# Two relus on ScalarE in place of a copy and a maximum, a fixed VectorE order for the last experts, and a shorter softmax for two tiles

## The chip, the cores and the metric

The kernel runs on one core of a Trainium2 chip. The metric is the time of one execution in microseconds of device time. The engines are called as in the profile: PE is TensorE (matmuls and transposes), PEld its weight load, DVE is VectorE, ACT is ScalarE, POOL is GpSimd, SP is SyncE, which issues most of the DMA transfers.

## The reference

Three stages follow each other: an attention with 4 sink columns and a window of 128, a dense layer with a leaky relu, and a layer of 8 experts of which each token uses one.

```python
scores = scale * np.matmul(q, k.transpose(0, 1, 3, 2))       # 2 x 8 heads, 768 tokens, 64 each; scale 1/8
scores = np.where(is_sink | in_window, scores, -1e9)
a = np.exp(scores - np.max(scores, axis=-1, keepdims=True))
a = a / (np.sum(a, axis=-1, keepdims=True) + 1e-9)
x = heads_together(np.matmul(a, v))                          # 1536 tokens x 512

h = x @ w_in                                                 # 512 -> 2048, weights arrive as float64
x = np.maximum(0.01 * h, h) @ w_out                          # 2048 -> 512

expert = np.argmax(x @ w_gate, axis=1)                       # 8 experts, at most 384 tokens each
h = np.maximum(x_e @ w1[e], 0.0)                             # 512 -> 1024
out = gate_weight * (h @ w2[e])                              # 1024 -> 512
```

## The kernel before

One program does all three stages, with the stages laid over each other.

**Attention.** The 1536 tokens are 12 tiles of 128. The first two tiles are "plain": for each of four units (a tile and a group of four heads) `qk_plain` (L630) transposes k and q on PE into one PSUM tile `kps`, copies q with ACT to `qp` (L640) and k with DVE to the two zero-padded halves `kz` (L643, two copies of 64 partitions). `scores_plain` (L646) multiplies them on top of a mask `mp`, takes the negated maximum of the raw scores on DVE (L662) and multiplies it with the scale (L663). `exps_plain` (L667) applies the scale inside the exponential (L674) and keeps the sums `su`. `norm_plain` (L679) makes 1/(su + 1e-9) on DVE for each half of the heads (L684, L685), and POOL multiplies the probabilities with it. The other ten tiles go through a class with a ring of keys: there DVE writes the mask into the scores (L538), takes the maximum (L539), makes the reciprocal of the sum (L220, L221) and prepares parts of q, k and the output (L148, L176, L196, L311), ACT makes the exponential (L213), POOL scales it (L223) and makes low parts (L148, L203, L232).

**Dense layer.** The class `FFN` works on 6 blocks of 256 tokens, each over 16 slices f of 128 hidden columns. `first` (L833) computes a slice hps in PSUM, `leak` (L845) applies the leaky relu, `second` (L867) adds the slice's part of the output into y. `second` of a slice is issued two slices later (`LAG` = 2). In block 0 the weights are still raw 8-byte words: for each f DVE turns two tiles of them (`rawi`, `rawo`) into fp32 tiles `cvt` with three operations each (L782, L786, L792), 96 conversions in all. `convert` gives them a lower priority than the rest, so they fill the gaps between the other DVE operations. The remaining attention tiles run during block 0. PSUM holds one buffer for hps, so `first` of the next slice begins when `leak` has read this one. Blocks 1 to 5 use split weights `wh` and `wl` that were made in block 0 (L812 on ACT, L813 on POOL).

`leak` in all blocks:

```python
g = self.p["g"].tile([P, N], F32, tag="g", name="g")
nc.scalar.activation(g, ps, AF.Copy, scale=0.01)              # L852
nc.vector.tensor_tensor(out=g, in0=ps, in1=g, op=ALU.max)     # L853
```

**Experts.** Tokens are scattered into `places` in DRAM by expert. For each group of at most 384 tokens the class `Experts` loads tokens `xg` and weights `craw`, splits the weights into high and low parts `cw` (L1140, L1142 and L1144), transposes tokens (`turn`, L1235), splits them (`x_parts`: L1241 on ACT, L1242 on DVE), copies gate weight and target row of each token from `xg` to `gt` (L1243, DVE, 128x2), and runs the two products (`up_one` L1272, `turn_one` L1286 to L1289, `down` L1299). `out` (L1302) multiplies with the gate weight (L1307) and POOL issues the indirect DMA (L1308). The groups that follow the first ones run under a test of the token count; the last four, with few tokens, run as `lone` (L1318), one after the other, in the arm at L1419 to L1424.

**Order.** PE, SP, ACT and POOL issue in program order (`ORDERED`, with `manual_schedule`). The order of DVE is set by a scheduler from priorities and its own estimate of readiness. Every engine takes its instructions strictly in the order that results.

Of the kernel before, what the change touches and what calls it, by code (L numbers as in the profile page):

```python
# [8 lines left out]
F32 = mybir.dt.float32  # L9
F32R = mybir.dt.float32r  # L10
BF16 = mybir.dt.bfloat16
I32 = mybir.dt.int32
AF = mybir.ActivationFunctionType
ALU = mybir.AluOpType
# [4 lines left out]
P = 128  # L19
# [3 lines left out]
ET = mybir.EngineType  # L23
ORDERED = {ET.PE, ET.SP, ET.Activation, ET.Pool}
# [363 lines left out]
class RingAttention(Attention):  # L388
# [16 lines left out]
    def setup(self):  # L405
        nc = self.nc
        c = self.p["ac"]
# [5 lines left out]
        fill = NEG  # L413
# [4 lines left out]
        for t in range(self.plain):  # L418

            m = self.p["c"].tile([P, (t + 1) * P], BF16, tag="c", name="mp")  # L420
            nc.gpsimd.memset(m, 0.0)
            for x in range(t + 1):
                self.keep_mask(m[:, x * P:(x + 1) * P], (t - x) * P, 0 if x else self.n_sink, fill / self.scale)
            self.mp.append(m)
            for g in range(self.NG):
                q = self.p["c"].tile([P, 2, P], F32, tag="c", name="qp")
                k = self.p["c"].tile([P, 2, 2, P], F32, tag="c", name="kz")
                for e in range(2):
                    nc.vector.memset(k[64 - 64 * e:128 - 64 * e, e], 0.0)
                self.qk[t, g] = q, k  # L430
# [200 lines left out]
    def qk_plain(self, t, g):  # L631


        nc = self.nc
        ps = self.p["ps"].tile([P, 4, P], F32, tag="att", name="kps")
        for n, (nm, pr) in enumerate(("kq"[n // 2], n % 2) for n in range(4)):
            x = self.heads(t, g, nm)[:, 2 * pr:2 * pr + 2, :]
            nc.tensor.transpose(ps[:, n, :], x.rearrange("p a d -> p (a d)"), self.ident)
        q, k = self.qk[t, g]
        nc.scalar.copy(q, ps[:, 2:4, :])  # L640
        for e in range(2):
            d = slice(64 * e, 64 * e + 64)
            nc.vector.tensor_copy(k[d, e], ps[d, 0:2, :])  # L643

    def scores_plain(self, t, g):

        nc = self.nc
        n = t + 1
        mx = self.p["sm"].tile([P, 2, 2], F32, tag="mx", name="mx")
        pss = []  # L650
        for e in range(2):
            if (t * self.NG + g) % 2:
                ps = self.p["psy"].tile([P, 2, n, P], F32, tag=f"y{e}", name="sps")
            else:
                ps = self.p[("psh", "psc")[e]].tile([P, 2, n, P], F32, tag="hu"[e], name="sps")
            for pr in range(2):
                for x in range(n):
                    nc.tensor.matmul(ps[:, pr, x, :], lhsT=self.ident_b, rhs=self.mp[t][:, x * P:(x + 1) * P],
                                     start=True, stop=False)
                    nc.tensor.matmul(ps[:, pr, x, :], lhsT=self.qk[t, g][0][:, pr, :],  # L660
                                     rhs=self.qk[x, g][1][:, e, pr, :], start=False, stop=True)
            nc.vector.reduce_max(mx[:, e, :], ps.rearrange("p a n c -> p a (n c)"), axis=AX.X, negate=True)  # L662
            nc.vector.tensor_scalar(out=mx[:, e, :], in0=mx[:, e, :], scalar1=self.scale, scalar2=None, op0=ALU.mult)  # L663
            pss.append(ps)
        self.pu[t, g] = (pss, mx)

    def exps_plain(self, t, g):  # L667
        pss, mx = self.pu[t, g]
        su = self.p["sm"].tile([P, 2, 2], F32, tag="su", name="su")
        pms = []  # L670
        for e, ps in enumerate(pss):
            pm = self.p["c"].tile([P, 2, (t + 1) * P], F32, tag="c", name="pm")
            for pr in range(2):
                self.nc.scalar.activation(pm[:, pr, :], ps[:, pr].rearrange("p n c -> p (n c)"), AF.Exp,  # L674
                                          bias=mx[:, e, pr:pr + 1], scale=self.scale, accum_out=su[:, e, pr:pr + 1])
            pms.append(pm)
        self.pu[t, g] = (pms, su)

    def norm_plain(self, t, g):  # L679
        nc = self.nc  # L680
        pms, su = self.pu[t, g]
        ri = self.p["sm"].tile([P, 2, 2], F32, tag="ri", name="ri")
        for e, pm in enumerate(pms):
            nc.vector.tensor_scalar(out=ri[:, e], in0=su[:, e], scalar1=1.0e-9, scalar2=None, op0=ALU.add)  # L684
            nc.vector.reciprocal(ri[:, e], ri[:, e])  # L685
            nc.gpsimd.tensor_tensor(out=pm, in0=pm, in1=ri[:, e].unsqueeze(2).to_broadcast(list(pm.shape)), op=ALU.mult)

    def trans_plain(self, t, g):
# [35 lines left out]
class FFN:  # L724
# [10 lines left out]
    N = 256  # L735
# [111 lines left out]
    def leak(self, j, f):  # L847

        nc, N = self.nc, self.N
        ps = self.g[j, f]  # L850
        g = self.p["g"].tile([P, N], F32, tag="g", name="g")
        nc.scalar.activation(g, ps, AF.Copy, scale=0.01)  # L852
        nc.vector.tensor_tensor(out=g, in0=ps, in1=g, op=ALU.max)  # L853
        self.g[j, f] = g

    def split_g(self, j, f, end=False):
# [204 lines left out]
class Experts:  # L1061
# [175 lines left out]
    def x_parts(self, gi, n, px):  # L1237

        nc, DM = self.nc, self.DM
        h, l = (self.xt[:, a, :, n * P:(n + 1) * P] for a in range(2))  # L1240
        nc.scalar.copy(h, px)  # L1241
        nc.vector.tensor_tensor(out=l, in0=px, in1=h.bitcast(F32), op=ALU.subtract)  # L1242
        nc.vector.tensor_copy(self.gt[gi % 4][n].bitcast(I32), self.xg[gi % 2][n][:, DM:DM + 2].bitcast(I32))  # L1243

    def up(self, e, h, f, u0, u1):

# [141 lines left out]
    def run(self):  # L1388
# [24 lines left out]
        tail = [gi for gi, (e, js) in enumerate(self.groups) if e >= self.short]  # L1413
# [3 lines left out]
        for a in names:  # L1417
            setattr(self, a, at[a] if isinstance(at[a], int) else at[a].copy())
        with self.tc.If(self.cnt[self.E] <= P, preferred_fallthrough_block=True) as c:  # L1419
            for gi in tail:  # L1420
                if self.groups[gi][1][0] == 0 and self.NH == 2:
                    self.lone(gi, self.fetch_one)
                else:
                    self.group(gi, int(self.groups[gi][1][0] == 0), 0)  # L1424
        for a in names:
            setattr(self, a, at[a])
        with c.Else():
# [4 lines left out]
def build(tc, A, n_sink, window, capacity):  # L1432
# [14 lines left out]
    with ExitStack() as es:  # L1447
# [150 lines left out]
        for j in range(NB):  # L1598
# [9 lines left out]
            for i, f in enumerate(ffn.order(j)):  # L1608
# [6 lines left out]
                if ndone < min(count, count * (i + 1) // (ffn.NF - 1)):  # L1615
                    step(leak)
                    ndone += 1
                else:
                    leak()
# [104 lines left out]
```

## Time and profile before

| | us |
|---|---|
| median of 3 runs | 640.67 |
| lowest and highest run | 638.81, 641.47 |
| profiled execution, its own time | 638.71 |
| span of that execution in the trace | 637.0 |

| engine | busy us | share of the span |
|---|---|---|
| PE | 594.7 | 93% |
| DVE | 431.0 | 68% |
| ACT | 342.6 | 54% |
| POOL | 232.9 | 37% |

The span is what the trace covers, the time has 1.7 us around it. The mean granted clock of PE is 0.991 of full speed. The shares are averages over stages that differ: the plain tiles end at about 38.5 us, block 0 of the dense layer lies from there to about 114 us, blocks 1 to 5 follow, and the four lone groups begin at about 574 us.

### The profile page before, as it was taken

The page shows a single profiled execution, that of the slowest core. Times are in us where ns is not written, and L with a number is a line of the kernel's source. Part 1 is how long each engine was busy: PE and PEld are TensorE (multiplying, and loading weights), DVE is VectorE, ACT ScalarE, POOL GpSimd, SP SyncE. Part 2 cuts the span into 40 slices and gives each one's busy share as a digit, 9 for nine tenths or more (in the row PEclk, how much of TensorE's full clock was granted, in tenths as well). Part 3 has the DMA queues.
Part 4 walks back from the last instruction along what each step waited for, and adds up shares of the span by engine and source line. Part 5 has one row for each costly group of instructions (what it writes and reads, how often), then busy time and mean ns, then how long its engine had stood idle before and what let it go on. Part 6 is the DMA issues. An engine that isn't in the chain of part 4 may idle for free.

```text
span 637.0 us, 12451 instructions
## 1 busy us (share of the span) xinstructions
PE 594.7 (93%) x4057; PEld 519.4 (82%) x4057; DVE 431.0 (68%) x1047; ACT 342.6 (54%) x997; POOL 232.9 (37%) x451
## 2 busy tenths in 40 slices
PE   8569888899999999999999999998999999997995
PEld 7457666679999999998999998986798888985774
DVE  5998999579976676667666662377466666556971
ACT  4546655777856566646665543264343444435741
POOL 5725556654464445535543453131101001010030
PEclk9988999999999999999999999999999999999999
DMA  8668889521445402140214006666257665437800
GB/s 240 160 201 244 267 221 288 154 84 51 176 145 169 127 17 69 38 139 8 62 32 132 2 31 209 218 206 196 92 166 232 215 201 177 150 120 225 278 14 13
DMA packets 83711, 91.83 MB, mean 144 GB/s; under 512 B 43171, under 2 KB 51363, under 8 KB 83616
## 3 DMA queue, kind: packets, MB, share of 16 engines
q1 hardware_dynamic: 81536, 85.58, 44.9%
q0 software_dynamic: 2080, 5.13, 2.2%
q8 instruction: 41, 0.67, 0.5%
q14 instruction: 54, 0.44, 0.2%
HBM read 71.91 MB, written 20.48 MB: 145 GB/s over the span
## 4 chain that ended last, share of the span: by engine, by line
PE 63%; DVE 17%; issue 10%; DMA 4%; ACT 4%; POOL 1%; another core or an unknown queue 0%; DVEq 0%; POOLq 0%; ACTq 0%
PE hps L844 16%; PE y L882 15%; PE py L1299 9%; PE ph L1252 8%; PE ops L300 4%; DMA out<-ys,gt 3%; DVE cvt L792 3%; PE sps L526 2%; DVE word L786 2%; DMA craw<-in_moe_w 2%; DVE word L782 2%; DVE g L853 1%; PE lps L965 1%; DVE cvt L786 1%; PE ph L1272 1%
## 5 line engine op out<-in xcount | busy, mean ns | idle before, releaser
L882 PE MATMUL y<-wh,gp 128*128 128x512 f32 x320 | 115.1, 400 | 1.4 <-ACT gp L862 1.4
L864 POOL TENSOR_TENSOR gp<-g,gp 128x256 fp32r<-128x256 f32 x77 | 56.8, 738 | 141.9 <-ACT gp L862 132.0
L844 PE MATMUL hps<-xth,wh 128*128 128x256 f32 x320 | 92.7, 290 | 0.0
L844 PE MATMUL hps<-xtl,wh 128*128 128x256 f32 x320 | 90.2, 282 | 0.0
L844 PE MATMUL hps<-xth,wl 128*128 128x256 f32 x320 | 90.0, 281 | 0.0
L1144 DVE TENSOR_TENSOR cw<-craw,cw 128x512 fp32r<-128x512 f32 x128 | 83.5, 697 | 8.7 <-ACT cw L1142 7.4
L1299 PE MATMUL py<-cw,ht 128*128 128x512 f32 x336 | 84.0, 403 | 4.5 <-DVE ht L1289 4.5
L1299 PEld LDWEIGHTS py<-cw,ht 128*128 128x128 f32 x336 | 63.0, 192 | 19.8 <-DVE ht L1289 6.2
L1142 ACT CAST cw<-craw 128x512 fp32r<-128x512 f32 x112 | 63.5, 621 | 28.1 <-PE py L1299 27.4
L1308 POOL DMA_INDIRECT out<-ys,gt x14 | 17.4, 1242 | 160.9 <-DVE ys L1307 146.5
L853 DVE TENSOR_TENSOR g<-hps,g 128x256 f32<-128x256 f32 x96 | 40.3, 419 | 52.4 <-ACT g L852 44.0
L852 ACT ACTIVATE g<-hps 128x256 f32<-128x256 f32 x96 | 36.4, 380 | 70.1 <-PE hps L844 70.0
L882 PEld LDWEIGHTS y<-wh,gp 128*128 128x128 f32 x320 | 60.0, 188 | 12.6 <-ACT gp L862 2.2
L844 PEld LDWEIGHTS hps<-xth,wh 128*128 128x128 f32 x320 | 60.3, 188 | 3.4 <-DVE g L853 0.7
L844 PEld LDWEIGHTS hps<-xtl,wh 128*128 128x128 f32 x320 | 60.3, 188 | 2.9 <-issue 0.5
L882 PE MATMUL y<-wl,gp 128*128 128x512 f32 x160 | 62.7, 392 | 0.0
L844 PEld LDWEIGHTS hps<-xth,wl 128*128 128x128 f32 x320 | 60.6, 189 | 0.0
L1252 PE MATMUL ph<-xt,cw 128*128 128x256 f32 (+2 forms) x444 | 58.2, 291 | 1.4 <-DVE xt L1242 0.9
L1252 PEld LDWEIGHTS ph<-xt,cw 128*128 128x128 f32 x444 | 56.6, 189 | 2.2 <-DVE xt L1242 1.6
L862 ACT CAST gp<-g 128x256 fp32r<-128x256 f32 x80 | 32.7, 409 | 39.0 <-DVE g L853 31.6
L213 ACT ACTIVATE pm<-pm,mx 128x132 f32<-128x132 f32 (+1 forms) x80 | 31.7, 398 | 30.7 <-DVE mx L539 30.4
L844 PE MATMUL hps<-xth,cvt 128*128 128x256 f32 x128 | 34.3, 415 | 8.2 <-DVE g L853 8.2
(205 smaller groups left out, 1282.0 us busy)
## 6 DMA issues: line engine op xcount, KB each, us to landing
craw<-in_moe_w SPq DMA_DIRECT2D x128, 256.0 KB
rawi<-in_moe_w_in SPq DMA_DIRECT2D x16, 512.0 KB
rawo<-in_moe_w_out SPq DMA_DIRECT2D x16, 512.0 KB
places<-zero SPq DMA_DIRECT2D x24, 257.0 KB
wh<-wscr SPq DMA_DIRECT2D x16, 256.0 KB
wl<-wscr SPq DMA_DIRECT2D x16, 256.0 KB
xg<-places SPq DMA_DIRECT2D x14, 257.0 KB
natv<-in_v SPq DMA_DIRECT2D x12, 256.0 KB
```

The lines of the kernel that those rows point to most:

```text
L213: nc.scalar.activation(pm[:, e, 0:w], pm[:, e, 0:w], AF.Exp, bias=mx[:, e:e + 1], accum_out=su[:, e:e + 1])
L300: nc.tensor.matmul(ps[:, e, :], lhsT=l, rhs=r, start=(x == 0), stop=(x == len(mm) - 1))
L844: nc.tensor.matmul(ps, lhsT=w, rhs=x, start=(n == 0), stop=(n == len(mm) - 1))
L852: nc.scalar.activation(g, ps, AF.Copy, scale=0.01)
L853: nc.vector.tensor_tensor(out=g, in0=ps, in1=g, op=ALU.max)
L862: nc.scalar.copy(gp[:, 0], g)
L864: eng.tensor_tensor(out=gp[:, 1], in0=g, in1=gp[:, 0].bitcast(F32), op=ALU.subtract)
L882: nc.tensor.matmul(y, lhsT=l, rhs=r, start=(start and n == 0), stop=(stop and n == len(mm) - 1))
L1142: nc.scalar.copy(h, t)
L1144: eng.tensor_tensor(out=l, in0=t, in1=h.bitcast(F32), op=ALU.subtract)
L1252: nc.tensor.matmul(self.ph[f][:, sl], lhsT=w, rhs=self.xt[:, a, k, sl], start=(m == 0), stop=(m == 3 * self.K - 1), skip_group_check=True)
L1299: nc.tensor.matmul(self.py[n], lhsT=x, rhs=w, start=(h == 0 and f == 0 and m == 0), stop=(h == self.NH - 1 and f == self.HF - 1 and m == 2))
```

## The change

Four edits.

1. **Plain tiles.** q is scaled when ACT copies it out of PSUM, so the scores are already scaled: the mask is filled with the plain value, the maximum is no longer multiplied (8 DVE operations 128x2 go) and the exponential has no scale. The k copy of the second half goes to ACT, ahead of the q copy; the first half stays on DVE. The sums' addition and reciprocal are made once for both halves (8 + 8 operations 128x2 become 4 + 4 of 128x4).
2. **Leaky relu of block 0.** ACT makes relu(h) and relu(-0.01 h) in two activations into a tile of the big pool, POOL subtracts the second from the first. DVE takes no part, and hps is released when ACT has read it twice.
3. **Gate copy.** `gt` is copied by POOL in place of DVE, in all groups.
4. **Last experts.** In the arm with the four lone groups DVE too issues in program order.

```diff
@@ qk_plain
-        nc.scalar.copy(q, ps[:, 2:4, :])
-        for e in range(2):
-            d = slice(64 * e, 64 * e + 64)
-            nc.vector.tensor_copy(k[d, e], ps[d, 0:2, :])
+        nc.vector.tensor_copy(k[0:64, 0], ps[0:64, 0:2, :])
+        nc.scalar.copy(k[64:128, 1], ps[64:128, 0:2, :])
+        nc.scalar.activation(q, ps[:, 2:4, :], AF.Copy, scale=self.scale)
@@ scores_plain
-            nc.vector.tensor_scalar(out=mx[:, e, :], in0=mx[:, e, :], scalar1=self.scale, scalar2=None, op0=ALU.mult)
@@ norm_plain
+        nc.vector.tensor_scalar(out=ri, in0=su, scalar1=1.0e-9, scalar2=None, op0=ALU.add)
+        nc.vector.reciprocal(ri, ri)
         for e, pm in enumerate(pms):
-            nc.vector.tensor_scalar(out=ri[:, e], in0=su[:, e], scalar1=1.0e-9, scalar2=None, op0=ALU.add)
-            nc.vector.reciprocal(ri[:, e], ri[:, e])
@@ leak
-        g = self.p["g"].tile([P, N], F32, tag="g", name="g")
-        nc.scalar.activation(g, ps, AF.Copy, scale=0.01)
-        nc.vector.tensor_tensor(out=g, in0=ps, in1=g, op=ALU.max)
+        if j == 0:
+            t = self.p["c"].tile([P, 2, N], F32, tag="c", name="gr")
+            g, r = t[:, 0], t[:, 1]
+            nc.scalar.activation(g, ps, AF.Relu)
+            nc.scalar.activation(r, ps, AF.Relu, scale=-0.01)
+            nc.gpsimd.tensor_tensor(out=g, in0=g, in1=r, op=ALU.subtract)
+        else:
+            ...
@@ x_parts
-        nc.vector.tensor_copy(self.gt[gi % 4][n].bitcast(I32), self.xg[gi % 2][n][:, DM:DM + 2].bitcast(I32))
+        nc.gpsimd.tensor_copy(self.gt[gi % 4][n].bitcast(I32), self.xg[gi % 2][n][:, DM:DM + 2].bitcast(I32))
@@ run
         with self.tc.If(self.cnt[self.E] <= P, preferred_fallthrough_block=True) as c:
-            for gi in tail:
+            with self.tc.manual_schedule(engines=ORDERED | {ET.DVE}):
+                for gi in tail:
                     ...
```

DVE in the plain stage, around the first conversions (L782, L786), in the order before; `kps` are the transposed q and k of the third and fourth unit, `su` the sums of earlier ones:

```order
L782 TENSOR_SCALAR cvt<-rawi 128x512
L782 TENSOR_SCALAR cvt<-rawo 128x512
L643 COPY kz<-kps 64x256 x2
L684 TENSOR_SCALAR ri<-su 128x2
L786 SCALAR_TENSOR_TENSOR cvt<-rawi,cvt 128x512
L685 RECIPROCAL ri<-ri 128x2
L662 TENSOR_REDUCE mx<-sps 128x2
```

The same place now (the lines of the changed kernel: L640 is the k copy, L661 the maximum, L681 and L682 sum and reciprocal, L780 and L784 the conversions):

```order
L661 TENSOR_REDUCE mx<-sps 128x2
L640 COPY kz<-kps 64x256
L661 TENSOR_REDUCE mx<-sps 128x2 x2
L681 TENSOR_SCALAR ri<-su 128x4
L682 RECIPROCAL ri<-ri 128x4
L780 TENSOR_SCALAR cvt<-rawi 128x512
L780 TENSOR_SCALAR cvt<-rawo 128x512
L784 SCALAR_TENSOR_TENSOR cvt<-rawi,cvt 128x512
L784 SCALAR_TENSOR_TENSOR cvt<-rawo,cvt 128x512
```

The last k copy, which stood behind two conversions, now stands ahead of all of them.

POOL in block 0, a stretch with the products for the attention (L223, L574, L232) and one split of weights (`wl`), before:

```order
L232 TENSOR_TENSOR pl<-pm,ph 128x264
L813 TENSOR_TENSOR wl<-cvt,wh 128x512
L223 TENSOR_TENSOR pm<-pm,ri 128x264
L574 AFFINE_SELECT pt<-pt 128x512 x2
L813 TENSOR_TENSOR wl<-cvt,wh 128x512
```

The same stretch now, with `gr` the tile of the two relus:

```order
L232 TENSOR_TENSOR pl<-pm,ph 128x264
...
L811 TENSOR_TENSOR wl<-cvt,wh 128x512
L223 TENSOR_TENSOR pm<-pm,ri 128x264
L855 TENSOR_TENSOR gr<-gr 128x256
L574 AFFINE_SELECT pt<-pt 128x512 x2
L811 TENSOR_TENSOR wl<-cvt,wh 128x512
```

The subtraction stands behind L223, which needs the reciprocal that DVE makes; both wait in POOL's order.

DVE in the first of the last four groups, before (`gt` the gate copy, `ht` the low part of the hidden rows, `cw` weights):

```order
L1243 COPY gt_0_6076<-xg_0_6070 128x2
L1144 TENSOR_TENSOR cw<-craw,cw 128x512 x4
L1140 CAST cw<-craw 128x512
L1144 TENSOR_TENSOR cw<-craw,cw 128x512 x3
L1289 TENSOR_TENSOR ht<-ph_6813,ht 128x4x128
L1243 COPY gt_0_6079<-xg_0_6067 128x2
L1144 TENSOR_TENSOR cw<-craw,cw 128x512 x4
L1289 TENSOR_TENSOR ht<-ph_6745,ht 128x4x128
```

The same place now:

```order
L1150 TENSOR_TENSOR cw<-craw,cw 128x512 x6
L1295 TENSOR_TENSOR ht<-ph_6813,ht 128x4x128
L1146 CAST cw<-craw 128x512
L1150 TENSOR_TENSOR cw<-craw,cw 128x512 x5
L1295 TENSOR_TENSOR ht<-ph_6745,ht 128x4x128
```

The second gate copy, which belongs to the group after the next and stood between the two `ht`, is gone from DVE.

## Rows read from the trace of the kernel before

**Rows 1.** The page's header.
```profile
span 637.0 us, 12451 instructions
```

**Rows 2.** Windows: start:end, length, busy (count) PE PEld DVE ACT POOL, clock, DMA, GB/s.
```profile
16.00:38.50 22.50, 12.98 (x108) 11.35 (x109) 22.11 (x44) 12.06 (x36) 13.46 (x42) 0.99 0.58 159
...
38.50:114.00 75.50, 63.47 (x352) 46.18 (x352) 68.56 (x148) 44.45 (x141) 39.89 (x68) 0.96 0.89 253
114.00:144.00 30.00, 30.00 (x190) 23.02 (x190) 20.03 (x48) 21.50 (x69) 19.27 (x34) 1.00 0.33 103
```

**Rows 3.** Waits in block 0: engine, line, releaser: us in all, times, longest.
```profile
PE hps L844 <- DVE g L853: 8.2, 5, 3.4
POOL pm L223 <- DVE ri L221: 6.8, 4, 3.8
DVE ri L220 <- ACT pm L213: 3.4, 4, 1.0
```

**Rows 4.** Plain stage in time order: start, us, instruction, count [idle before <- releaser].
```profile
18.39 0.86 DVE L643 COPY kz<-kps 64x256 f32<-64x256 f32 x2
18.85 0.49 PE L660 MATMUL sps<-kz,qp 128*128 128x128 f32 x2 [3.15 <-DVE kz L643]
```

**Rows 5.** Groups of lines, plain stage: count | busy us, mean ns | idle before.
```profile
L684 DVE TENSOR_SCALAR ri<-su 128x2 f32<-128x2 f32 x8 | 1.7, 212 | 0.0
L685 DVE RECIPROCAL ri<-ri 128x2 f32<-128x2 f32 x8 | 1.3, 159 | 0.1
L663 DVE TENSOR_SCALAR mx<-mx 128x2 f32<-128x2 f32 x8 | 1.3, 163 | 0.1
L640 ACT COPY qp<-kps 128x256 f32<-128x256 f32 x4 | 1.5, 386 | 5.2 <-PE kps L638 5.2
```

**Rows 6.** Groups of lines in block 0.
```profile
L853 DVE TENSOR_TENSOR g<-hps,g 128x256 f32<-128x256 f32 x12 | 5.0, 419 | 1.2 <-ACT g L852 1.2
L220 DVE TENSOR_SCALAR ri<-su 128x2 f32<-128x2 f32 x8 | 3.2, 402 | 3.4 <-ACT pm L213 3.4
L176 DVE SCALAR_TENSOR_TENSOR qs<-natq,qs 128x256 fp32r<-128x256 f32 x4 | 1.7, 417 | 0.0
L148 DVE TENSOR_TENSOR ks<-natk,ks 128x256 fp32r<-128x256 f32 x1 | 0.5, 454 | 0.0
L852 ACT ACTIVATE g<-hps 128x256 f32<-128x256 f32 x13 | 5.0, 384 | 19.0 <-PE hps L844 19.0
L203 POOL TENSOR_TENSOR vt<-natv,vt 128x256 fp32r<-128x256 f32 x6 | 4.4, 734 | 9.1 <-ACT vt L202 9.1
```

**Rows 7.** DVE in block 0, in order of time.
```profile
76.44 0.69 DVE L786 SCALAR_TENSOR_TENSOR word<-rawi,word 128x512 int32<-128x512 int32 x1
77.04 0.42 DVE L853 TENSOR_TENSOR g<-hps,g 128x256 f32<-128x256 f32 x1
77.38 0.68 DVE L792 SCALAR_TENSOR_TENSOR cvt<-rawi,word 128x512 int32<-128x512 int32 x1
...
100.58 1.13 DVE L220 TENSOR_SCALAR ri<-su 128x2 f32<-128x2 f32 x1
...
103.93 0.69 DVE L786 SCALAR_TENSOR_TENSOR word<-rawo,word 128x512 int32<-128x512 int32 x1
104.66 0.69 DVE L792 SCALAR_TENSOR_TENSOR cvt<-rawo,word 128x512 int32<-128x512 int32 x1
```

**Rows 8.** DVE and PE in the last groups, in order of time.
```profile
584.82 0.17 DVE L1243 COPY gt<-xg 128x2 int32<-128x2 int32 x1 [4.72 <-DMA xg<-places]
...
573.73 4.35 PE L1272 MATMUL ph<-cw,xt 128*128 128x512 f32 x18
...
588.08 3.88 PE L1299 MATMUL py<-cw,ht 128*128 128x512 f32 x10 [3.99 <-DVE ht L1289]
591.80 4.37 PE L1272 MATMUL ph<-cw,xt 128*128 128x512 f32 x18
...
604.82 4.37 PE L1272 MATMUL ph<-cw,xt 128*128 128x512 f32 x18
```

More of the change, by code (lines that the diff above doesn't have):

```diff
@@ L422, in setup @@
             for x in range(t + 1):
-                self.keep_mask(m[:, x * P:(x + 1) * P], (t - x) * P, 0 if x else self.n_sink, fill / self.scale)
+                self.keep_mask(m[:, x * P:(x + 1) * P], (t - x) * P, 0 if x else self.n_sink, fill)
             self.mp.append(m)
@@ L674, in exps_plain @@
                 self.nc.scalar.activation(pm[:, pr, :], ps[:, pr].rearrange("p n c -> p (n c)"), AF.Exp,
-                                          bias=mx[:, e, pr:pr + 1], scale=self.scale, accum_out=su[:, e, pr:pr + 1])
+                                          bias=mx[:, e, pr:pr + 1], accum_out=su[:, e, pr:pr + 1])
             pms.append(pm)
@@ L850, in leak @@
         ps = self.g[j, f]
-        g = self.p["g"].tile([P, N], F32, tag="g", name="g")
-        nc.scalar.activation(g, ps, AF.Copy, scale=0.01)
-        nc.vector.tensor_tensor(out=g, in0=ps, in1=g, op=ALU.max)
+        if j == 0:
[5 more added lines that the diff above has]
+        else:
+            g = self.p["g"].tile([P, N], F32, tag="g", name="g")
+            nc.scalar.activation(g, ps, AF.Copy, scale=0.01)
+            nc.vector.tensor_tensor(out=g, in0=ps, in1=g, op=ALU.max)
         self.g[j, f] = g
@@ L1419, in run @@
         with self.tc.If(self.cnt[self.E] <= P, preferred_fallthrough_block=True) as c:
-            for gi in tail:
[L1421 to L1424, printed above, removed]
+            with self.tc.manual_schedule(engines=ORDERED | {ET.DVE}):
+                for gi in tail:
+                    if self.groups[gi][1][0] == 0 and self.NH == 2:
+                        self.lone(gi, self.fetch_one)
+                    else:
+                        self.group(gi, int(self.groups[gi][1][0] == 0), 0)
         for a in names:
```

## The prediction

> **What bounds the kernel now.** I read the windows first, stage by stage. In the plain stage from 16.0 us on, DVE works 22.11 of 22.50 us while PE works 12.98; in block 0 of the dense layer DVE works 68.56 of 75.50 us and PE 63.47; in the next 30 us PE works all 30.00 and DVE 20.03 [rows 2]. So up to about 114 us the end is set by DVE, which has to get through the weight conversions, and later by PE. A microsecond that DVE loses before 114 us is a microsecond of the program as long as PE, ACT and POOL can follow; one that it loses later is worth something only where PE waits for DVE.
>
> The waits in block 0 come second. PE waits 8.2 us in 5 pieces for the maximum in the leaky relu, L853 [rows 3]: the single buffer of hps is held until DVE comes to it. The reader is to see that DVE is both busy and late there. The timelines come third: in the plain stage PE stands 3.15 us for a k copy that DVE made only after two conversions [rows 4], and in the last groups PE stands 3.99 us once, because DVE had stopped 4.72 us at a gate copy whose tokens had not landed [rows 8].
>
> All sums are made against the profiled execution: span 637.0 us [rows 1], its own time 638.71 us. The median of the runs is 640.67, so 1.96 us are added at the end.
>
> **Plain stage.** Removed from DVE: 8 scalings of the maximum of 163 ns, 1.3 us; 4 of 8 additions of 212 ns and 4 of 8 reciprocals of 159 ns, 1.5 us; 4 of the 8 k copies, of which two take 0.86 us, so 1.7 us [rows 4, 5]. That is 4.5 us, the upper bound. Before 16 us DVE is not full, and there the parts lie beside waits for PE and ACT. From 16.0 on only the last unit's share counts: two k copies, 0.86 (one vanishes, the other moves ahead of the conversions), two scalings, 0.33, and a good half of the saved additions and reciprocals, 0.8: together 2.0 us. Against it stands ACT: each unit adds one more copy there, 0.39 us by the q copy [rows 5], and three readers of one PSUM tile now follow each other, so the first unit's chain is no shorter: the lower bound is 0. The added copies hide elsewhere, since ACT is busy 12.06 of 22.50 us [rows 2]; without this cover they would cost 4 times 0.39, 1.5 us. I take **2.0 us**, because the conversions behind it run back to back.
>
> **Leaky relu of block 0.** Twelve maxima of 419 ns leave the busy part of DVE, 5.0 us, with 1.2 us in which DVE waited for ACT in front of them [rows 6]: upper bound 6.2 us. Lower bound from the spacing: L786 to L792 is 0.73 us from start to start when nothing stands between, and 0.94 us with a maximum between them [rows 7], so that one costs only 0.21, as it fills a gap in a dependent pair; 12 times 0.21 is 2.5 us. Beyond this it can give less: the operations that then come up earlier on DVE depend on others. L220 has already waited 3.4 us for ACT in 4 pieces [rows 3], and that work doesn't get shorter. Two new waits of 0.6 us, half of the 1.2 that fell away, would take 1.2; so I keep 0 to 6.2 for the range and take **3.0 us**, nearer the low end, because most maxima stand between conversions.
>
> What covers it: ACT gets 13 more activations of 384 ns, 5.0 us, on 44.45 busy us of 75.50; POOL gets 13 subtractions, priced by the nearest row, L203 on 128x256, at 734 ns, 9.5 us on 39.89 [rows 2, 6]. Both then have over 20 us left. PE has 12 us idle in the stage, of which 8.2 are the waits for L853 [rows 2, 3]; hps would now be free after two activations, 0.77 us, where it was one activation and one maximum, 0.80, plus DVE's queue. PE therefore follows. The DMA share is 0.89 [rows 2]; DVE nowhere waits for a transfer there, so it may fall behind only a little.
>
> Here a page speaks against the change. The trace has a relu-like read of hps at 384 ns on ACT and 419 ns on DVE, for the same 128x256 [rows 6], so moving it costs ACT no more than DVE paid. The Trainium skill, ScalarE: Activation LUTs, section "Rules for kernel authors", says to use VectorE and not ScalarE for relu and max, VectorE being up to about 3 times faster per element in bf16. By that rule the two relus would be estimated at 2.5 us per slice and this term at nothing, some 3 us less in all; this case's data are fp32 out of PSUM, and its rows do not show it.
>
> **Gate copy and the last groups.** The gate copy of 0.17 us itself counts for nothing: PE is full there, and POOL is idle. What counts is its place. In the order before, the copy for the group after the next stands between the two `ht` of the first group, and DVE stops at it. The starts of the groups' first product on PE are 573.73, 591.80 and 604.82, so 18.07 and then 13.02 us apart [rows 8]. Without the stop and with DVE in program order the first group should take 13.0 too: **5.0 us**. Bounds: 4.0 (the 3.99 us for which PE itself waits) and 5.1. On POOL the copy waits for the same transfer, but in program order it stands one group later, ahead of only the output DMA.
>
> Sum: 2.0 + 3.0 + 5.0 = 10.0 us. The profiled execution would go from 638.71 to 628.7, the median from 640.67 to **630.7 us**.
>
> **The rivals.**
> 1. *Only the tail gains.* DVE gets faster up to 114 us, but what it then waits for (L213 on ACT, the hps on PE, transfers at a DMA share of 0.89) comes no sooner. For it: DVE's waits for ACT of 3.4 us [rows 3]. Against: PE's 8.2 us of waiting for DVE in the same stage. 640.67 - 5.0 = 635.7. Chance 0.14.
> 2. *The tail does not gain.* The wait for the tokens comes back on POOL, or DVE, now fixed in order, stops at a weight that has not landed. For it: DVE had the freedom to reorder. Against: the second group ran 13.02 us with the same work. 640.67 - 2.0 - 3.0 = 635.7. Chance 0.09.
> 3. *POOL slows DVE.* L220 takes 402 ns on average, and one of them 1.13 us [rows 6, 7], though the plain stage's L684 of the same size takes 212 [rows 5]; so something beside DVE stretches small operations. Thirteen operations of DVE in block 0 (8 L220, 4 L176, one L148) read only on-chip memory; if each were held for one more POOL operation of 734 ns, this costs 9.5 us, and eats the first two terms and nearly all of the third: 640.67 - 10.0 + 9.5 = 640.2, no change. Against: the mean excess of L220 is now 0.2 us with POOL busy half of the time, not 0.7. Chance 0.06. The Trainium skill, SBUF — State Buffer, section "SBUF: two separate sides", has a rule of this kind: DVE and GpSimd share a port pair under an exclusive lock, and the loser fully blocks.
> 4. *The subtraction comes too late (slower).* It stands in POOL's order behind L223, which waits up to 3.8 us for DVE [rows 3]. `second` needs it two slices later; with 75.50 us for 16 slices [rows 2] that is 9.4 us of slack. Relus (0.77), subtraction (0.73) and that wait (3.8) make 5.3 us. It decides from 4.1 us of further queue on POOL in front of it. If POOL were late by 1.5 us beyond the slack at each of 14 slices, PE would lose 21 us and block 0 grow; the maxima are still gone: 640.67 - 10.0 + 21 = 652. Against: POOL is idle 35 of 75.50 us. Chance 0.04.
>
> **How the numbers follow.** The forecast has 0.67. A measurement of this kernel can tell about 0.5%, 3.2 us, from no change: faster is below 637.5, slower above 643.9. Faster: the forecast and rivals 1 and 2, 0.67 + 0.14 + 0.09 = 0.90; same: rival 3, 0.06; slower: rival 4, 0.04. The range goes from all upper bounds less a wait or two, 640.67 - 4.5 - 6.2 - 5.1 = 624.9, to the tail-only case with a run's scatter of 1 us: **624.9 to 636.7**. Rivals 3 and 4 lie outside it, 0.10, and I leave about another tenth for misses of the terms.
>
> **What would show it.** The page of the changed kernel should list the maximum of `leak` 80 times instead of 96 and 16 subtractions on POOL; the conversions should end near 109 us in place of 114, and the first block-0 matmul start near 36.5 in place of 38.5; PE should wait for ACT and not for DVE at hps, and for less than 8.2 us; the starts of the four groups should be 13.0 us apart throughout. I would be wrong if DVE shows waits for POOL or transfers in block 0, if `second` waits for the subtraction, or if PE idles in the first of the four groups again.

## The result and the profile after

The changed kernel took 631.91 us as the median of 4 runs (630.34 to 633.91), the kernel before 639.75 us over 4 runs. The ratio is 0.9876, with a 95% interval of 0.9838 to 0.9914: faster by 7.8 us from median to median, where 10.0 were forecast. A second set of runs gave 632.88 us against 638.79, ratio 0.9901 (0.9879 to 0.9924). Both medians lie inside the stated range of 624.9 to 636.7 us. The profiled execution of the changed kernel is the slowest of its four runs: 633.91 us, span 632.0, with a mean granted clock of PE of 0.986, where the fastest run had 0.991. So the two traces differ by 5 us only, and the text below says where the rest is.

The windows of the changed kernel, with the columns of [rows 2]:

```profile
16.00:38.50 22.50, 16.08 (x116) 14.00 (x114) 22.20 (x35) 13.00 (x36) 13.68 (x42) 0.92 0.61 168
36.00:110.00 74.00, 64.58 (x357) 46.88 (x356) 66.87 (x138) 48.96 (x158) 49.25 (x82) 0.97 0.92 260
110.00:140.00 30.00, 29.93 (x179) 22.08 (x178) 16.78 (x41) 21.06 (x66) 20.52 (x34) 0.96 0.33 96
```

The order of the engines is as before: DVE sets the end up to 110 us, PE after it. In block 0 POOL went from 39.89 to 49.25 busy us, ACT from 44.45 to 48.96, as the working had it. But the clock share in the last row is 0.96 where it was 1.00 [rows 2].

The waits of the changed kernel in block 0 (36 to 112 us), with the columns of [rows 3]:

```profile
DVE ri L220 <- ACT pm L213: 4.1, 4, 1.0
...
PE hps L842 <- ACT gr L854: 2.4, 2, 2.2
...
PE ops L300 <- POOL pt L574: 2.2, 4, 1.4
```

PE's 8.2 us of waiting for the maximum are gone, with 2.4 us for the relus in their place. A wait is new: PE stands 2.2 us for an operation of POOL (L574, the mask of the transposed probabilities), which now queues behind the subtractions. Nothing waits for the subtraction itself in the second product. DVE's only wait for POOL there is 0.3 us at L538, right behind the last conversion.

The groups of the changed kernel in the same stretch answer to [rows 6]:

```profile
L176 DVE SCALAR_TENSOR_TENSOR qs<-natq,qs 128x256 fp32r<-128x256 f32 x5 | 3.8, 768 | 0.0
...
L220 DVE TENSOR_SCALAR ri<-su 128x2 f32<-128x2 f32 x8 | 2.0, 247 | 4.1 <-ACT pm L213 4.1
```

```profile
L853 ACT ACTIVATE gr<-hps 128x256 f32<-128x256 f32 x13 | 5.1, 392 | 8.9 <-PE hps L842 8.9
L854 ACT ACTIVATE gr<-hps 128x256 f32<-128x256 f32 x13 | 5.1, 391 | 0.0
...
L855 POOL TENSOR_TENSOR gr<-gr 128x256 f32<-128x256 f32 x13 | 9.5, 733 | 8.7 <-ACT gr L854 8.7
```

A relu costs what the scaled copy cost (392 and 391 against 384 ns), and the subtraction is 733 ns, at the price taken from L203.

PE ahead of block 0 and the last conversion on DVE in the kernel before:

```profile
37.33 0.51 PE L157 MATMUL kps<-ident_r,ks 128*128 128x128 f32 x4 [2.82 <-DVE kT L163]
...
113.74 0.69 DVE L792 SCALAR_TENSOR_TENSOR cvt<-rawo,word 128x512 int32<-128x512 int32 x1
```

The timelines of the changed kernel, first PE ahead of block 0, then DVE at its end, then PE at the starts of the four last groups, which answer to [rows 8]:

```profile
35.19 0.50 PE L157 MATMUL kps<-ident_r,ks 128*128 128x128 f32 x4 [2.92 <-DVE kT L163]
```

```profile
107.43 1.39 DVE L196 CAST qT<-qps 64x512 fp32r<-64x512 f32 x2 [0.52 <-ACT qT L193]
108.85 0.69 DVE L790 SCALAR_TENSOR_TENSOR cvt<-rawo,word 128x512 int32<-128x512 int32 x1
```

```profile
572.79 4.35 PE L1278 MATMUL ph<-cw,xt 128*128 128x512 f32 x18
...
585.79 4.35 PE L1278 MATMUL ph<-cw,xt 128*128 128x512 f32 x18
...
598.82 4.37 PE L1278 MATMUL ph<-cw,xt 128*128 128x512 f32 x18
...
611.83 4.34 PE L1278 MATMUL ph<-cw,xt 128*128 128x512 f32 x18
```

The first row stood at 37.33 us before: the plain stage gives 2.14 us. The last conversion ends at 109.54 us (108.85 + 0.69), where it ended at 114.43 (113.74 + 0.69): 4.89 us less, so the leaky relu gives the other 2.75. The four groups start 13.00, 13.03 and 13.01 us apart, where the first took 18.07. But the first of them starts at 572.79 instead of 573.73, only 0.94 us earlier: 3.95 of the 4.89 us that were there at 109 us had gone by then.

The losses are in the rows. The four matmuls of the second product right behind the last conversion, in the kernel before and in the changed one:

```profile
114.23 1.88 PE L882 MATMUL y<-cvt,g 128*128 128x512 f32 x4
```

```profile
109.54 3.35 PE L888 MATMUL y<-cvt,gr 128*128 128x512 f32 x4
```

and the windows of the changed kernel around them and at the end of the dense layer:

```profile
100.00:110.00 10.00, 7.46 (x46) 5.47 (x45) 7.71 (x17) 5.62 (x20) 4.55 (x10) 0.95 1.15 274
110.00:120.00 10.00, 10.00 (x48) 6.71 (x47) 3.86 (x9) 5.40 (x19) 7.96 (x13) 0.88 0.50 155
430.00:440.00 10.00, 8.67 (x49) 6.71 (x48) 7.84 (x16) 5.13 (x12) 0.61 (x2) 1.00 0.64 193
440.00:450.00 10.00, 9.00 (x46) 7.11 (x45) 4.50 (x28) 1.68 (x6) 1.20 (x2) 0.83 0.17 56
```

The same four matmuls take 3.35 us in place of 1.88, 1.5 us more, since PE ran part of 100 to 120 us at 1.2 GHz (shares 0.95 and 0.88), where the kernel before had 2.4 GHz throughout. The second fall is at 440 to 450 us (0.83); instruction for instruction, PE's lead over the kernel before shrinks from 2.7 to 1.5 us there. Ahead of both PE had been waiting: 1.04 us for L196 just before 109 us, and 0.64, 0.69 and 0.92 us between 434 and 443 us. These waits alone do not make a fall. The kernel before has them too, 1.04 us and then 0.70, 0.70 and 0.92 us, and its clock share is 1.00 in every window from 110 to 580 us:

```profile
113.76 0.64 PE L526 MATMUL sps<-kT,qT 128*128 128x264 f32 x3 [1.04 <-DVE qT L196]
...
445.43 0.18 PE L996 MATMUL pps<-roh,before 128*128 128x8 bf16 x1 [0.92 <-DVE rsl L980]
```

A smaller loss lies at the very end. PE's last matmuls, in the kernel before and in the changed one:

```profile
625.67 4.44 PE L1299 MATMUL py<-cw,ht 128*128 128x512 f32 x18
```

```profile
619.58 4.43 PE L1305 MATMUL py<-cw,ht 128*128 128x512 f32 x18
```

PE ends 6.1 us earlier (624.01 against 630.11), but the span ends only 5.0 us earlier. From PE's end to the span's end it is 6.4 to 6.9 us in all seven kept traces whose gate copy is on DVE, and 7.6 to 8.0 us in all seven whose gate copy is on POOL. So edit 3 costs about 1.1 us there. The excess comes behind the issue of the last output transfer; what takes this time is open.

### The profile page after: what moved, and what is told of

It is laid out like the page before. It is cut to its first block, busy times and chain, and to the rows that moved or that the text cites. A ratio compares the mean times of both kernels' runs of the same rounds, so it can differ in the third digit from the quotient of the medians.

```text
span 632.0 us, 12472 instructions
## 1 busy us (share of the span) xinstructions
PE 598.1 (95%) x4057; PEld 521.2 (82%) x4057; DVE 421.8 (67%) x997; ACT 348.2 (55%) x1017; POOL 244.7 (39%) x481
## 5 line engine op out<-in xcount | busy, mean ns | idle before, releaser
L1314 POOL DMA_INDIRECT out<-ys,gt x14 | 14.3, 1022 | 156.6 <-DVE ys L1313 151.5
L859 DVE TENSOR_TENSOR g<-hps,g 128x256 f32<-128x256 f32 x80 | 33.6, 419 | 49.2 <-ACT g L858 38.9
L858 ACT ACTIVATE g<-hps 128x256 f32<-128x256 f32 x80 | 30.3, 379 | 47.6 <-PE hps L842 47.5
L300 PEld LDWEIGHTS ops<-pt,vt 128*64 128x64 f32 x456 | 35.2, 135 | 7.7 <-POOL pt L574 5.2
```

Of the source, the lines that this page charges most:

```text
L300: nc.tensor.matmul(ps[:, e, :], lhsT=l, rhs=r, start=(x == 0), stop=(x == len(mm) - 1))
```

## The experiments

Each kernel was timed beside the kernel before on the same chip. Two of them add ten matmuls that nothing reads, and one makes a subtraction twice.

**Only the two relus.** Edit 2 alone.

```diff
 leak, on the kernel before
+        if j == 0:
             ...
+            nc.scalar.activation(g, ps, AF.Relu)
+            nc.scalar.activation(r, ps, AF.Relu, scale=-0.01)
+            nc.gpsimd.tensor_tensor(out=g, in0=g, in1=r, op=ALU.subtract)
+        else:
             ...
```

> Only the leaky relu of block 0 is changed (two relus on ACT, subtraction on POOL). Theory (VectorE time is the bound in block 0): the last conversion ends about 2.75 us earlier than the 114.4 us of the kernel before, the time falls by about 2.5 us to some 637.5, below what the timing alone can tell. Rival (early release of hps is the gain): the same here, to be told apart by a kernel that frees hps early and leaves the maximum on VectorE. Rival (what comes next eats it): conversions end at 114 as before, time 640.

638.05 us over 10 runs against 640.14 over 22: ratio 0.9959 (0.9935 to 0.9982). Its last conversion on DVE:

```profile
111.02 0.69 DVE L792 SCALAR_TENSOR_TENSOR cvt<-rawo,word 128x512 int32<-128x512 int32 x1
```

It ends at 111.71 us, 2.72 earlier than before. The term is right in size, and its place too; by the ratio the time falls by 0.4%, 2.6 us.

**Only the plain tiles.** Edit 1 alone.

```diff
 qk_plain, on the kernel before (with the mask, the maximum, the exponential and the reciprocal as in the change)
+        nc.vector.tensor_copy(k[0:64, 0], ps[0:64, 0:2, :])
+        nc.scalar.copy(k[64:128, 1], ps[64:128, 0:2, :])
+        nc.scalar.activation(q, ps[:, 2:4, :], AF.Copy, scale=self.scale)
         ...
```

> Only the two plain tiles are changed. Theory: the weight conversions run about 2.1 us earlier from 35 us on and end near 112.2 instead of 114.4, time about 638. Rival (the gain is lost again before block 0 ends, because the attention or PE sets the pace): conversions end at 114, time 640. Slower rival (the k copy on ACT delays the first chain): the first matmul of block 0 comes later than 38.5 us.

643.77 us over 10 runs against 640.14: ratio 1.0046 (1.0021 to 1.0072). It is slower, which no line of the expectation had. The conversions did end early, at 111.08 us (110.39 + 0.69):

```profile
110.39 0.69 DVE L790 SCALAR_TENSOR_TENSOR cvt<-rawo,word 128x512 int32<-128x512 int32 x1
```

Right behind them PE's clock fell (0.83 from 110 to 120 us), as in the changed kernel. More was lost 330 us later. The windows, and DVE and PE around 517 us:

```profile
440.00:450.00 10.00, 9.00 (x43) 7.44 (x41) 4.15 (x24) 1.19 (x5) 1.18 (x2) 0.73 0.21 70
...
460.00:470.00 10.00, 8.82 (x59) 8.21 (x59) 5.00 (x11) 3.50 (x7) 0.98 (x1) 0.83 0.66 210
```

```profile
514.05 0.75 DVE L1305 TENSOR_SCALAR ys<-py,gt 128x512 f32<-128x512 f32 x1 [1.19 <-PE py L1297]
...
517.87 0.24 DVE L1241 COPY gt<-xg 128x2 int32<-128x2 int32 x2 [3.06 <-issue]
518.01 0.68 DVE L1240 TENSOR_TENSOR xt<-ph,xt 128x512 fp32r<-128x512 f32 x1
...
518.75 2.49 PE L1250 MATMUL ph<-xt,cw 128*128 128x128 f32 x14 [1.35 <-DVE xt L1240]
```

PE's clock falls at 440 and 460 us, in a stretch whose instructions are those of the kernel before. And DVE stands 3.06 us at 517 us between two groups, ahead of the gate copy, where the kernel before stands 1.53 us. In the last groups the gate copy stops DVE for 5.54 us, not 4.72.

**Only the gate copy on POOL, and only the fixed order.** Edits 3 and 4, each alone.

```diff
 x_parts (first kernel)
+        nc.gpsimd.tensor_copy(self.gt[gi % 4][n].bitcast(I32), self.xg[gi % 2][n][:, DM:DM + 2].bitcast(I32))
 run (second kernel)
+            with self.tc.manual_schedule(engines=ORDERED | {ET.DVE}):
```

> Only the gate copy goes from VectorE to POOL; VectorE's order in the last four groups stays with the scheduler. Theory (the stop at the hoisted copy is all): the first of the four groups takes 13.0 us instead of 18.07, time about 635. Rival (the fixed order is what helps): the first group still takes over 15 us, time 638 or more.

> Only VectorE's order in the last four groups is fixed to program order; the gate copy stays on VectorE, behind the token split of its own group. Theory (the stop at the hoisted copy is all): the first group takes 13.0 us instead of 18.07, time about 635, as with the copy on POOL. Rival (the copy must leave VectorE): the stop moves but stays, the first group takes over 15 us, time 638 or more.

The gate copy alone: 635.0 us over 5 runs, ratio 0.9899 (0.9864 to 0.9933). The order alone: 634.65 us over 6 runs, ratio 0.9915 (0.9881 to 0.9950). PE's starts of the first three of the last groups, with the gate copy on POOL, then with the order fixed:

```profile
573.15 4.34 PE L1272 MATMUL ph<-cw,xt 128*128 128x512 f32 x18
...
586.15 4.35 PE L1272 MATMUL ph<-cw,xt 128*128 128x512 f32 x18
...
599.20 4.35 PE L1272 MATMUL ph<-cw,xt 128*128 128x512 f32 x18
```

```profile
574.41 4.34 PE L1272 MATMUL ph<-cw,xt 128*128 128x512 f32 x18
...
587.40 4.35 PE L1272 MATMUL ph<-cw,xt 128*128 128x512 f32 x18
...
600.49 4.37 PE L1272 MATMUL ph<-cw,xt 128*128 128x512 f32 x18
```

Both groups take 13.0 us. Either edit removes the stop by itself; the other then adds nothing there. What cost 5 us was the place that the scheduler gave to a copy of 0.17 us.

**The changed kernel again, and without its plain part.**

```diff
 second kernel, on the changed kernel: mask, qk_plain, scores_plain, exps_plain and norm_plain as before
```

> The changed kernel, unaltered, for a second profile and more runs on the chip that runs the others. Theory (the parts add up, and what is missing of the forecast 10 us went into stretches at half clock on PE): conversions end near 109.5 us again, the four last groups are 13.0 us apart again, and the time differs from run to run with the granted clock; ratio to before 0.985 to 0.991. Rival (a loss of the program's own between 110 and 490 us, such as POOL's gate copy): the same loss at the same places in this profile, whatever the clock.

> The changed kernel without its part for the plain tiles. Theory (the plain part gives 2 to 3 us up to the end of the conversions, and that reaches the end): conversions end near 112 us, the time is 2 to 3 us above that of the whole change, some 633. Rival (the plain part costs by itself more than it gives, as it did when it was alone, 643.8 against 640.1): the time is below that of the whole change by 2 us or more, some 628.

The whole change: 632.88 us over 6 runs, ratio 0.9901. Without the plain part: 633.73 us over 6 runs, ratio 0.9914 (0.9892 to 0.9936). The intervals overlap; the plain part is worth 0.8 us, which these runs cannot tell from nothing. In the second profile of the whole change PE's clock falls at the same places:

```profile
100.00:110.00 10.00, 7.47 (x46) 5.33 (x45) 7.71 (x17) 5.61 (x20) 4.55 (x10) 0.96 1.12 260
110.00:120.00 10.00, 10.00 (x48) 6.73 (x47) 3.98 (x9) 5.25 (x18) 7.92 (x13) 0.87 0.52 164
...
440.00:450.00 10.00, 9.00 (x45) 7.18 (x44) 4.49 (x26) 1.68 (x6) 1.19 (x2) 0.83 0.17 61
```

So the falls at 109 and 443 us came in two executions. Without the plain part the conversions end at 112.18 us, 2.64 later, and the clock is 1.00 from 100 to 120 us:

```profile
111.98 1.88 PE L890 MATMUL y<-cvt,gr 128*128 128x512 f32 x4
```

The four matmuls end at 113.86 us; in the changed kernel they end at 112.89. Of 2.64 us on DVE 0.97 are left on PE, 1.5 having gone with the fall at 109 us, and at 485 us nothing is left. The fall near 443 us is there without the plain part too (0.83 from 440 to 450 us).

**Early release alone.** ACT frees hps as in the change, DVE still makes the maximum, now of two on-chip tiles.

```diff
 leak, on the kernel before, block 0
             ...
+            nc.scalar.activation(g, ps, AF.Copy)
+            nc.scalar.activation(r, ps, AF.Copy, scale=0.01)
+            nc.vector.tensor_tensor(out=g, in0=g, in1=r, op=ALU.max)
```

> Against the kernel before, only block 0's leaky relu: ACT copies hps twice (once times 0.01) and so frees it as early as two relus do, but VectorE still makes the maximum, of two on-chip tiles. Theory (VectorE's time is what counted): conversions end within 1 us of the 114.4 us of before, time 640. Rival (early release of hps is the gain): conversions end near 111.7 us, as with the two relus alone.

643.61 us over 5 runs against 638.79: ratio 1.008 (1.0043 to 1.0117). The conversions end at 117.84 us, 3.4 later than before, outside of both expectations. The group of its maximum:

```profile
L857 DVE TENSOR_TENSOR gr<-gr 128x256 f32<-128x256 f32 x12 | 10.0, 837 | 0.8 <-ACT gr L856 0.7
```

The maximum costs 837 ns on average in block 0 (from 419 to 1460 over all 16), where it was 419 with one operand in PSUM [rows 6]. PE's wait at hps fell from 8.2 to 2.8 us, and the kernel is slower all the same: releasing hps early is not enough. DVE's maxima took 5.0 us more and the conversions ended 3.4 later, which speaks for DVE's time as what counted. It is no clean price of either, since both were changed at once and PE's clock fell here at 72 us too (0.66 from 70 to 80 us). The Trainium skill, SBUF — State Buffer, section "SBUF: two separate sides", says that a DVE operation with two on-chip inputs and a GpSimd operation that reads on-chip memory exclude each other, the later one blocking fully. The trace agrees with it: three of the twelve in block 0 have no POOL operation beside them and take 420 ns, and the longest, 1460 ns, begins beside a split of weights on POOL (L813); the maximum of the kernel before, with an input in PSUM, did not show it.

**POOL's subtraction twice.**

```diff
 leak, on the changed kernel, block 0
+            nc.gpsimd.tensor_tensor(out=self.p["g"].tile([P, N], F32, tag="g", name="spare"), in0=g, in1=r, op=ALU.subtract)
             nc.gpsimd.tensor_tensor(out=g, in0=g, in1=r, op=ALU.subtract)
```

> The changed kernel with POOL's subtraction in block 0 made twice, once into a spare tile: 16 more POOL operations of some 0.74 us. Theory (POOL has room and does not hold up VectorE): conversions end within 1 us of 109.5, time within 2 us of the changed kernel. Rival (POOL's operations stretch VectorE's small ones): 13 operations stretched by up to 0.7 us more, conversions end 2 us or more later. Slower rival (the subtraction comes too late for the second product): PE waits for the subtraction and block 0 ends 5 us or more later.

637.22 us over 10 runs, ratio 0.9977 (0.9961 to 0.9993), 4.3 us above the whole change on the same chip. The conversions end at 114.32 us (113.63 + 0.69), 4.8 later. The theory that POOL had room falls. Waits in block 0:

```profile
PE ops L300 <- POOL pt L574: 6.7, 9, 3.0
...
DVE pm L538 <- ACT pm L531: 2.6, 2, 1.4
...
DVE xtl L311 <- ACT xth L305: 1.4, 1, 1.4
```

POOL is busy 57.40 of 78.00 us, so it has room in total. But it works in order: the mask L574 comes later, PE waits 6.7 us for it at the attention's last product (2.2 in the changed kernel, none before), ACT gets its inputs later, and DVE waits 4.0 us at L538 and L311 that it did not wait before. DVE's small operations are not longer for it (L220 243 ns, L176 680), so a stretch is not the cause. Of the 4.0 us only the 1.4 at L311, at 73 us, follow such a wait of PE directly, the longest (3.0 us). The other two stand behind stretches of PE at half clock: 1.2 us at 41 us, which the filled kernel below has as well, without a second subtraction, and 1.4 us at 78 us, after a fall at 72 us. So the queue's delay is shown, but how much of the 4.8 us is the queue's and how much the clock's is not.

**Filling PE's waits.** Ten matmuls into an unused tile where PE waited between 434 and 443 us, on the changed kernel, and on the plain part alone.

```diff
+        def fill(n):
+            for _ in range(n):
+                nc.tensor.matmul(junk, lhsT=ident, rhs=ident, start=True, stop=True)
         while pending:
             ...
+            fill(3)
             second()
 ...
         routing = route(ts[:-1])
+        routing.insert(2, lambda: fill(4))
```

> The changed kernel with ten extra transposes-sized matmuls into an unused PSUM tile, three ahead of each of the last two dense slices and four ahead of the router's first ranking matmul, where PE waited 0.64, 0.69 and 0.92 us near 434.6, 437.0 and 442.5 us. Theory (PE's clock falls after these waits, and the half-clock stretch near 443.6 us costs the program): the stretch is gone, PEclk reads 1.00 from 440 to 450 us, and the time is 1 to 2 us below the changed kernel's 632.9, some 631. Rival (the stretch has nothing to do with PE's waits there): PEclk falls there again and the time is the same or up to 1 us longer.

> Only the plain tiles are changed, and PE's waits at the end of the dense layer are filled with the same ten extra matmuls. Theory (the plain part alone was slower only because PE's clock fell from 444 us on): PEclk is 1.00 from 440 to 450 us, the time is 637 to 639, below the kernel before. Rival (the plain part costs by itself): about 643 us again.

On the changed kernel: 634.59 us over 6 runs, ratio 0.9898 (0.9857 to 0.9938), so no gain over the change's 0.9901. The windows:

```profile
440.00:450.00 10.00, 9.92 (x62) 8.10 (x61) 5.74 (x35) 2.27 (x7) 1.20 (x2) 1.00 0.19 66
...
460.00:470.00 10.00, 10.00 (x74) 10.00 (x74) 5.31 (x11) 3.37 (x8) 0.00 (x0) 0.83 0.42 134
470.00:490.00 20.00, 19.49 (x113) 17.06 (x113) 12.93 (x23) 8.74 (x17) 3.09 (x4) 0.96 0.69 212
```

The fall at 440 us is gone with the waits, and another at 460 us and one at 488 us have come. The clock's loss moved. That the filling is what moved it is not shown: the fall at 109 us is gone in this profile as well (1.00 from 100 to 120 us, the four matmuls take 1.88 us), although nothing is altered before 434 us. On the plain part alone: 643.89 us over 10 runs against 641.35, ratio 1.0037 (1.0005 to 1.0069). There too the clock is 1.00 from 440 to 490 us (it falls to 0.83 in 510 to 530), and the kernel is no faster for it: DVE's stop between two groups is there again, 3.25 us at 516 us, and PE waits 2.69 us for it. So the clock was not the only reason why the plain part alone is slow.

**The kernel before again.**

> The kernel before, unaltered, for a second profile. Theory (where the clock falls belongs to the program, as it did twice at 109 and 443 us in the changed kernel): half-clock stretches near 38 and 48 us, where VectorE is the bound, none from 110 to 580 us. Rival (where it falls is chance): it falls at other places, between 430 and 520 us too.

639.34 us over 10 runs of the same program gave a ratio of 0.9975 (0.9938 to 1.0012) to the other runs of itself, which shows what a measurement can tell. In its profile PE's clock falls at 18, 49 and 66 us, while DVE is the bound, and at 588 us, around the stop in the last groups; it is 1.00 from 110 to 580 us, as in the first profile of this kernel. The exact places in the first 70 us differ, though the program is the same.

**Plain part and gate copy on POOL.**

```diff
 on the kernel before: the plain tiles' edits and the gate copy on POOL
```

> The plain tiles' part and the gate copy on POOL, nothing else. Alone, the plain part was 3 us slower than the kernel before (twice), with VectorE stopped 3.1 and 3.3 us at a gate copy near 517 us, where the kernel before did not stop. Theory (the plain part is slower alone only because of gate copies on VectorE): no such stop, PE starts the four last groups 13.0 us apart, and the time is that of the gate copy alone or up to 2 us less, 633 to 635 beside a before of 640. Rival (the plain part costs by itself): 3 us above the gate copy alone, 638 or more.

On another chip than the others, 636.99 us over 12 runs against 639.45 over 17: ratio 0.9961 (0.9938 to 0.9983), between the two expectations. The four groups are 13.0 us apart, but the stop between two groups stays, now ahead of another instruction:

```profile
509.15 0.75 DVE L1305 TENSOR_SCALAR ys<-py,gt 128x512 f32<-128x512 f32 x1 [1.24 <-issue]
512.95 0.69 DVE L1240 TENSOR_TENSOR xt<-ph,xt 128x512 fp32r<-128x512 f32 x1 [3.05 <-ACT cw L1140]
...
513.70 5.56 PE L1250 MATMUL ph<-xt,cw 128*128 128x128 f32 x32 [1.41 <-DVE xt L1240]
```

The theory that a gate copy on VectorE was what stopped it falls. The token split had its input from ACT at 511.65 us and started 1.3 us later. The stop of 3.05 to 3.25 us stands in all three kernels that have the plain part without the relus, and in none of the others (2.0 us at most there); it comes behind `ys` at the change of groups, whichever instruction is next, and in two of the three the profile names nothing that was waited for ("issue"). What holds DVE there is open; it was not tried further. One rival that the traces leave standing is the transfer of instructions: the DMA queues named "instruction" move four or five packets in these microseconds, in the kernel before too.

## Why the prediction was right, and where a step failed

**Right.** The time, its direction and the range. The plain stage: 2.0 us forecast, 2.14 measured up to block 0. The leaky relu: 3.0 forecast, 2.75 in the whole change and 2.72 alone at the end of the conversions, near the lower bound of 2.5 as argued. The first of the last groups: 5.0 forecast, 5.07 measured from start to start (18.07 to 13.00). The end of the conversions was put near 109 us and is 109.54; the first matmul of block 0 near 36.5 and is 36.2.

**What was luck in it.** One profile does not give the end of the conversions this closely. Kernels with the same edits in block 0 ended them at 113.90, 114.43, 114.85 and 115.37 us (none), 111.08, 112.85 and 114.35 (plain), 111.71 and 112.18 (relus), and 109.52, 109.54 and 111.26 (both). The means bear the two terms out, 1.9 us for the plain part and 2.7 for the relus; that the first pair of profiles fits to a few tenths is chance. And the range holds more than the forecast: rival 1 with 635.7 us and the gate copy alone with 635.0 lie in it too.

**The step that failed** is the first one: "A microsecond that DVE loses before 114 us is a microsecond of the program as long as PE, ACT and POOL can follow". The forecast counted 5.0 us for the plain stage and the relus together. They were there at the last conversion (4.89), and 0.94 were left at 573 us in the profiled execution. PE followed, but for part of 100 to 120 and of 440 to 450 us at 1.2 GHz, where it ran at 2.4 before: 1.5 us on four matmuls, and 1.2 us at 443. These two places came again in a second profile. The rest went in smaller steps. The plain part is the one that lost most: 2.64 us at the conversions, 0.97 four matmuls later, 0.8 in the time. The clock column of the windows shows it, and the working had no term for it.

All fourteen kept traces bear this out. From the last conversion to the first product of the last groups it takes 459.0 to 460.1 us in the five whose clock share is 1.00 all the way (the kernel before twice, the gate copy alone, the order alone, early release). It takes 460.7 to 468.6 us in the nine whose clock falls on the way, three of which also have the stop of DVE; the changed kernel takes 463.3 and 463.0. Why the clock falls in one kernel and not in another stays open.

**The cover that was thinner than said.** "Both then have over 20 us left" is right for the sums (POOL 49.25 of 74.00) and wrong as a measure of slack. POOL's order put the mask L574 behind the subtraction, and PE waits 2.2 us that it did not wait before. With a second subtraction the conversions ended 4.8 us later, in part by this queue. Rival 4 looked at the wrong reader: not the second product waits, with its 9.4 us of slack, but the attention's.

**The rivals.** Rival 1, only the tail gains, is half of what happened: the tail's 5.0 came whole (about 1.1 us were lost at the end again), the rest shrank, for another reason than it named. Rival 2 did not happen: POOL's gate copy waited for nothing, and DVE in program order stopped at no weight. Rival 3's price did not come about. L220 fell from 402 to 247 ns (1.2 us less over 8) and L176 rose from 417 to 768 (1.8 us more over 5), so the stretching moved from one operation to another with little in sum; no run shows whether it was POOL that stretched these two. The rule quoted beside it, from the Trainium skill, SBUF — State Buffer, section "SBUF: two separate sides", fits the maximum of two on-chip tiles in the early-release kernel (837 ns); the change avoids that by giving the whole operation away.

**The rule on relu.** The rule of the Trainium skill, ScalarE: Activation LUTs, section "Rules for kernel authors", would have made the relus' term nothing, by the prediction's estimate. ACT's relus took 392 and 391 ns beside a maximum of 419 on VectorE, and the term is 2.7 us: here, on fp32 out of PSUM, the rule does not decide.

**How the parts add up.** By the ratios: relus 0.4%, the gate copy or the order 0.9 to 1.0%, relus with both 0.9%, all four 1.0 to 1.2%. The plain part costs 0.4 to 0.5% alone and gives 0.1% with the others, less than the interval. No kernel tried was clearly faster than the whole change. Nor is the whole change clearly faster than the gate copy alone, a change of one line: 0.9876 to 0.9901 beside 0.9899 (0.9864 to 0.9933). What these runs show in the time is the tail's term, and 0.4% for the relus alone; of the other 5.0 us about 1 reached the last groups in the profiles.

## What to carry to other kernels

An engine that is the bound of one stage gives back what is taken from it only if the next bound runs the same afterwards; read PE's granted clock window by window in both kernels before a saving is counted to the end. Slack of an in-order engine is the wait of the next reader behind the new instruction, not its idle time. A tiny operation that a scheduler hoists above a late transfer can cost thirty times its own length, and moving it to an idle engine or fixing the order removes the stop equally well; only the first cost 1.1 us elsewhere here. Where profiles of one program differ by microseconds at the place that is read, several of them are needed for each term.

## What was not expected of the hardware

PE's clock fell at the same two places in two executions of the changed kernel, and stayed at 2.4 GHz from 110 to 580 us in two of the kernel before, which has the same waits of PE there. But with ten idle matmuls added from 434 us on it fell at neither place, not even at 109 us, where nothing was altered. So neither the program nor the waits of PE alone fix the places. The same maximum on VectorE doubled, from 419 to 837 ns, when its PSUM operand became an on-chip one beside a busy POOL. And twenty DVE instructions removed in the first 35 us went, in the three kernels that had this without the relus, with a stop of DVE of 3 us at a change of groups 480 us later, whose cause stayed open.
